# Gated MLP forward on one core: the row-tile and chunk order, the layer norm and a guard pass put in a hand-written order

## The chip, the cores and the metric

One core of a Trainium2 chip. The metric is the device time of one execution in microseconds (us), taken as the median of repeated runs. Engines in the text: PE (matrix multiply; PEld is its weight load), DVE (vector), ACT (scalar, with activation tables), POOL and SP. DMAs are issued by SP (one queue) and by POOL (another), and both queues are served by the core's 16 DMA engines.

## The reference

The forward and backward pass of a block over 2048 rows of width D = 576. Only the first stage of the kernel is touched by the change. What the whole computes:

```python
xn = layernorm(x)                                  # 2048 x 576, eps 1e-5
s  = attention(xn, k_cache, v_cache, wq, wo)       # 32 heads of 128, 2048 keys
h  = sigmoid(xn @ w_gate) * (xn @ w_up)            # F = 4608
g  = silu(h @ w_down)
out = x + s * g
# and the gradients with respect to x, k_cache, v_cache, wq, wo,
# w_gate, w_up, w_down for a given grad_out
```

Everything is bfloat16 in memory; matmuls accumulate in float32.

## The kernel before

**The whole.** The program runs in stages: layer norm and the gate and up projections of the MLP (the stage of this change), the down projection with the derivative of the silu (L425 and following), attention head by head forward and backward, then the weight gradients and the gradient of x. The first stage ends at 377.5 us of the profiled execution, and the down projection follows.

**The tiling of the first stage.** 2048 rows are NT = 16 row tiles of 128. D = 576 is DT = 5 contraction tiles of 128; the last is padded: only 64 rows of it hold data, and the 64 low partitions of the weights' last tile are zeroed (`zlow`, L128, by POOL). F = 4608 is NFC = 9 chunks of 512 columns (`FCH`). For one row tile and one chunk PE runs five matmuls into `g_ps` (L363) and five into `u_ps` (L365), each of 128x512; ACT makes `a_row` = sigmoid(g) (L366), DVE makes `h_row` = u * a (L369). Call this a step. `g_ps` and `u_ps` have three PSUM buffers each. GRP = 3 chunks form a group; there are three groups, and in each the loop runs over all 16 row tiles. At the end of a row tile in a group POOL writes `h_row` and `a_row` (128 x 1536, three buffers each) to `h_d` and `a_d` in HBM (L371, L372).

**Layer norm.** `ln_tile(st)` (L327 to L341) is called two row tiles ahead within the first group. For each row tile it runs the statistics on DVE (L331, L333), a square root on ACT (L335), reciprocal and bias on DVE (L336, L339), the normalization on ACT, in place in `x_all` (L340), five transposes on PE (L58), and a copy of the result into `xnT`, in turn on DVE (L42) and ACT (L40). The square root and the sigmoid lie in different activation tables, and a change between them appears as ACT_TABLE_LOAD in the trace.

**Loads.** SP loads row tiles 0 and 1 of x (L303), then for chunk 0 the five contraction tiles of both weights (L314, L315, ten DMAs), then the other 14 row tiles (L317), then the rest of the weights in column ranges of up to 1536. POOL stores the normalized rows to `xn_d` (L351) and loads the down weights `wd_sb` (L352); in the program both stand at the last row tile of the first group.

**The guard.** The attention stage has a fast path that is valid only if the keys and `wq` are small. A guard computes sums of squares: it loads 84 pieces of 128x1024 (64 of `A_k_cache`, 20 of `wq`) into the space of `x_all`, nine slots, and squares and sums each, odd pieces on ACT (L265), even ones on DVE (L267). `guard_step` issues the load of piece k on SP and the square of piece k - GLA, with GLA = 5. It is called once in each step of the second and third group, between the sigmoid and the product:

```python
                            nc.scalar.activation(a_row[:, cs], g_ps[:], AF.Sigmoid)
                            if grp > 0:
                                guard_step()
                            nc.vector.tensor_tensor(h_row[:, cs], u_ps[:], a_row[:, cs], op=ALU.mult)
```

`guard_end` (L282 to L296) reduces the sums over the partitions through a small tensor in HBM and sets a flag.

**What sets the order.** The order within each engine is not that of the program: a scheduler reorders instructions by priority where dependencies allow. The trace shows it: `wd_sb` is issued at 8.96 us, and the guard's squares begin at 113 us, before the last row tile of the first group is through. Dependencies between engines, and reuse of buffers, are semaphore waits, placed by the framework.

## Time and profile before

| | us |
|---|---|
| median of 5 runs | 5120.81 (5105.55 to 5129.96) |
| the profiled execution | 5134.45 |
| its span, first to last instruction | 5131.7 |
| PE busy | 4952.4 (97%) |
| end of the first stage in it | 377.5 |
| mean granted TensorE clock | 0.99 |

The profile is of one execution. Busy times are sums over instructions; the ends of matmuls are modelled, so a busy PE isn't PE at its peak. In the rows of waits the columns are: who waited for whom, us in total, times, the longest. In the rows of DMA issues: tensors, queue, count, KB of each, and the median us from issue to landing. In the rows by stretch of time each engine has its busy us and its number of instructions.

### The profile page before, as it was taken

To read this page: it belongs to the slowest core of one execution; us is meant where nothing else is said; L and a number is where in the kernel's file an instruction comes from. 1 tells how busy PE (TensorE), PEld (TensorE's weight loads), DVE (VectorE), ACT (ScalarE), POOL (GpSimd) and SP (SyncE) were. 2 spreads that over 40 slices of the span, in tenths; PEclk is the share of its full clock that TensorE was granted. 3 is DMA by queue.
4 is the path that set the end of the run, shared out by engine and by line. 5 is a ranking of instruction groups with operands and counts; after the bars stand their busy time and mean duration, and the time that the engine had idled before them with its cause. 6 is when DMAs were issued, how large, how long until landed. Compare 5 with 4: busy or idle time off the path is not lost.

```text
span 5131.7 us, 127940 instructions
## 1 busy us (share of the span) xinstructions
PE 4952.4 (97%) x53585; PEld 3487.5 (68%) x54480; DVE 2585.8 (50%) x6734; ACT 2602.6 (51%) x4663; POOL 896.6 (17%) x1370
## 2 busy tenths in 40 slices
PE   8899999999999999999999999999899999999999
PEld 3345677777778777777777877777746666555554
DVE  4534556656666666665665666666525444200111
ACT  6521666666667666666666766666513333211000
POOL 1112111111111111111111111111112222211000
PEclk8999999999999999999999999999999999999999
DMA  7648999999999999999999999999986665797976
GB/s 271 234 147 195 177 198 212 208 205 208 206 201 208 214 206 208 206 208 201 215 212 194 211 215 205 209 202 203 210 205 188 188 190 183 221 262 179 174 142 122
DMA packets 2756960, 1031.35 MB, mean 201 GB/s; under 512 B 2663761, under 2 KB 2667986, under 8 KB 2756370
## 3 DMA queue, kind: packets, MB, share of 16 engines
q1 hardware_dynamic: 2659490, 699.97, 73.2%
q0 software_dynamic: 96880, 323.05, 19.3%
q8 instruction: 427, 7.00, 0.6%
q14 instruction: 163, 1.34, 0.1%
HBM read 175.31 MB, written 182.13 MB: 70 GB/s over the span
## 4 chain that ended last, share of the span: by engine, by line
PE 79%; issue 10%; DMA 7%; DVE 2%; POOL 2%; ACT 1%; SPq 0%; POOLq 0%; DVEq 0%; ACTq 0%
PE acc L623 15%; PE acc L564 14%; PE acc L855 12%; PE sp L517 7%; PE acc L1026 6%; PE acc L212 5%; PE dp L587 5%; PE dh L908 3%; PE acct L145 2%; PE u_ps L365 2%; DMA out_dram<-kvo 2%; PE g_ps L363 2%; PE acc L425 2%; PE acc L826 2%; DMA x_all<-in_A_k_cache_dram 1%
## 5 line engine op out<-in xcount | busy, mean ns | idle before, releaser
L535 ACT ACTIVATE Pq<-sp 128x1024 bf16<-128x1024 f32 x1024 | 1048.0, 1024 | 317.7 <-PE sp L517 203.9
L623 PEld LDWEIGHTS <-Pq 128*128 128x128 bf16 x16384 | 1004.9, 98 | 241.8 <-issue 3.4
L594 ACT ACTIVATE t<-dp,negdelta 128x1024 bf16<-128x1024 f32 x512 | 571.6, 1116 | 222.1 <-PE dp L587 168.8
L590 DVE SCALAR_TENSOR_TENSOR Pq<-dp,negdelta,Pq 128x1024 bf16<-128x1024 f32 x512 | 655.0, 1279 | 42.4 <-PE acc L564 38.7
L564 PEld LDWEIGHTS <-PT 128*128 128x128 bf16 x8192 | 502.5, 98 | 129.9 <-DMA PT<-Pq 8.2
L587 PE MATMUL dp<-VT,dOT 128*128 128x512 bf16 x1728 | 542.8, 381 | 32.6 <-DVE Pq L590 32.4
L564 PE MATMUL acc<-Vn,PT 128*128 128x128 bf16 x8192 | 547.5, 219 | 14.6 <-DMA PT<-Pq 7.8
L564 PE MATMUL acc<-Kn,dST 128*128 128x128 bf16 x8192 | 551.6, 219 | 9.4 <-DMA dST<-Pq 5.8
L623 PE MATMUL acc<-dOn,Pq 128*128 128x128 bf16 x8192 | 547.0, 219 | 10.1
L517 PE MATMUL sp<-KQ 128*128 128x512 bf16 x1762 | 548.3, 380 | 2.9 <-ACT Pq L535 2.8
L623 PE MATMUL acc<-Qn,Pq 128*128 128x128 bf16 x8192 | 542.9, 220 | 3.4
L564 PEld LDWEIGHTS <-dST 128*128 128x128 bf16 x8192 | 492.5, 98 | 68.3 <-DMA dST<-Pq 7.6
L595 DVE TENSOR_TENSOR Pq<-t,Pq 128x1024 bf16<-128x1024 bf16 x512 | 354.3, 692 | 359.0 <-ACT t L594 352.2
L604 ACT ACTIVATE dq_n<-acc,rsc 128x128 bf16<-128x128 f32 x512 | 188.3, 368 | 336.7 <-PE acc L564 336.7
L1042 DVE SCALAR_TENSOR_TENSOR junk<-acc,xn_all 128x512 f32<-128x512 f32 (+1 forms) x32 | 13.9, 453 | 642.9 <-ACT dxn L1041 642.9
L637 POOL DMA_DIRECT2D out_dram<-kvo x256 | 140.4, 548 | 1036.5 <-DVE kvo L635 1031.2
L558 POOL DMA_DIRECT2D on_d<-o_n x128 | 97.1, 759 | 741.4 <-DVE junk L576 391.5
L1041 ACT ACTIVATE dxn<-acc 128x512 f32<-128x512 f32 (+1 forms) x32 | 12.8, 406 | 399.6 <-PE acc L1026 392.1
L910 DVE TENSOR_TENSOR du_blk<-dh,ah 128x256 bf16<-128x256 f32 x288 | 120.4, 418 | 188.1 <-PE dh L908 186.0
L635 DVE SCALAR_TENSOR_TENSOR kvo<-acc,part 128x512 bf16<-128x512 f32 x256 | 175.9, 687 | 65.8 <-DMA out_dram<-kvo 37.1
L50 DVE TENSOR_SCALAR o_n<-acc,rinv_all 128x128 bf16<-128x128 f32 x352 | 123.2, 350 | 168.2 <-PE acc L564 168.2
L522 DVE TENSOR_REDUCE rs_all<-rsp 128x1 f32<-128x2 f32 x512 | 78.0, 152 | 256.3 <-ACT Pq L535 254.0
(198 smaller groups left out, 6989.8 us busy)
## 6 DMA issues: line engine op xcount, KB each, us to landing
out_dram<-kvo POOLq DMA_DIRECT2D x256, 128.0 KB, 4.1
h_d<-h_row POOLq DMA_DIRECT2D x48, 384.0 KB, 3.0
a_d<-a_row POOLq DMA_DIRECT2D x48, 384.0 KB, 2.6
ah<-a_d POOLq DMA_DIRECT2D x18, 1024.0 KB, 7.0
ah<-h_d POOLq DMA_DIRECT2D x18, 1024.0 KB, 9.9
du_d<-du_blk POOLq DMA_DIRECT2D x18, 1024.0 KB, 8.7
dg_d<-dg_blk POOLq DMA_DIRECT2D x18, 1024.0 KB, 10.4
x_all<-in_A_k_cache_dram SPq DMA_DIRECT2D x64, 256.0 KB, 6.2
```

The costliest lines, as they stand in the source:

```text
L212: nc.tensor.matmul(av[:, :CH], lhsT=w[:, i, :], rhs=srcT[:, i, cs], start=(i == 0), stop=(i == DT - 1))
L517: nc.tensor.matmul(sp[:, c * CH:(c + 1) * CH], lhsT=hs.QT[:, qt * P:(qt + 1) * P], rhs=hs.KT[:, hf * HW_ + c * CH: hf * HW_ + (c + 1) * CH ...
L535: nc.scalar.activation(Pq[:, hsl], sp[:], AF.Exp, scale=SCALE, accum_out=hs.rsp[:, hf:hf + 1])
L564: nc.tensor.matmul(hs.acc[:, 0, :], lhsT=T[:, kt, :], rhs=rhs[:, kt, :], start=(kt == 0), stop=(kt == NT - 1))
L587: nc.tensor.matmul(dp[:, c * CH:(c + 1) * CH], lhsT=hs.dOT[:, qt * P:(qt + 1) * P], rhs=hs.VT[:, hf * HW_ + c * CH: hf * HW_ + (c + 1) * C ...
L590: nc.vector.scalar_tensor_tensor(Pq[:, hsl], dp[:], hs.negdelta[:, qt:qt + 1], Pq[:, hsl], op0=ALU.add, op1=ALU.mult)
L594: nc.scalar.activation(t[:], dp[:], AF.Identity, bias=hs.negdelta[:, qt:qt + 1], scale=1.0)
L595: nc.vector.tensor_tensor(Pq[:, hsl], t[:], Pq[:, hsl], op=ALU.mult)
L604: nc.scalar.activation(hs.dq_n[:, qt % G4, :], hs.acc[:, 0, :], AF.Copy, scale=hs.rsc[:, qt:qt + 1])
L623: nc.tensor.matmul(self.tile[:, j, :], lhsT=self.slabs[qt][:, kt * P:(kt + 1) * P], rhs=self.rhs[:, qt, :], start=(qt == self.lo), stop=(q ...
L855: nc.tensor.matmul(accs[j][:, :nn], lhsT=lhs[:, st, cols], rhs=rhs[:, st, n0:n0 + nn], start=(st == 0), stop=(st == NT - 1))
L1026: nc.tensor.matmul(self.accs[sl][j][:, :nn], lhsT=ch[:, kk, sl * P:(sl + 1) * P], rhs=wT[:, k0 + kk, n0:n0 + nn], start=(self.k + kk == 0) ...
```

## The change

The nine chunks are walked in five groups: chunk 0 alone, then the pairs (1,2), (3,4), (5,6), (7,8); each group runs over all 16 row tiles. The weights are loaded in the same groups, with one DMA for the four full contraction tiles of a weight and one for the padded one. Seven row tiles of x are loaded (in three DMAs) ahead of the first weights. The zeroing of the padding is split: the first 512 columns on DVE, the rest on POOL.

The layer norm is taken apart into `bn` (statistics), `rstd` (root, reciprocal, bias for a range of row tiles), `norm`, `turn` (transposes) and `put_T` (copy). Roots are taken three times: for row tiles 0 and 1, 2 to 6, and 7 to 15. The block is in `tc.manual_schedule()`: the instructions of each engine keep the order of the program. `xn_d` and `wd_sb` are issued after the first group. The row buffers are 128x1024, four of each.

The guard's ticks are spread over the 128 steps of the pairs, ending 14 steps before the last, with GLA = 7; the square now stands after the product of the step. `guard_end` is split: `guard_reduce`, with the DMAs, follows the last tick.

```diff
@@ -129,7 +129,8 @@
 
     FCH = min(512, F)
     NFC = F // FCH
-    GRP = ldiv(NFC, 3)
+    NB2F = ldiv(NFC - 1, 2) if NFC > 1 else 1
+    groups1 = [(0, 1)] + [(c, c + NB2F) for c in range(1, NFC, NB2F)]
 
     acc_box = [None]
     heads_pre = {}
@@ -238,7 +239,7 @@
         GQ = NT * P // 2
         NGW = -(-HD // GQ)
         NGS = NT * D // GQ
-        GLA = min(5, NGS - 1)
+        GLA = min(7, NGS - 1)
         pieces = [("k", h, hf) for h in range(H) for hf in range(2)] + [("w", i, c) for i in range(DT) for c in range(NGW)]
...
@@ -278,7 +279,9 @@
 
         x_flat = [None]
 
-        def guard_end():
+        gr_box = []
+
+        def guard_reduce():
             gm = gp.tile([P, 2], f32, name="gm", bufs=1)
             ks = gp.tile([P, H], f32, name="ks", bufs=1)
             nc.vector.tensor_reduce(ks[:], ksq[:].rearrange("p (h a) -> p h a", a=2), axis=AX.X, op=ALU.add)
@@ -288,6 +291,10 @@
             nc.sync.dma_start(gd_d[1:2, :].rearrange("o p -> p o"), gm[:, 1:2])
             gr = gp.tile([1, 2, P], f32, name="gr", bufs=1)
             nc.sync.dma_start(gr[:], gd_d[:, :].rearrange("(o a) p -> o a p", o=1))
+            gr_box.append(gr)
+
+        def guard_end():
+            gr = gr_box[0]
             gs = gp.tile([1, 4], f32, name="gs", bufs=1)
             nc.vector.tensor_reduce(gs[:, 0:1], gr[:, 0, :], axis=AX.X, op=ALU.max)
             nc.vector.tensor_reduce(gs[:, 1:2], gr[:, 1, :], axis=AX.X, op=ALU.add)
@@ -299,79 +306,133 @@
         x_all = a0x.tile([P, NT, D], bf, name="x_all")
         x_flat[0] = x_all[:].rearrange("p t d -> p (t d)")
         with tc.tile_pool(name="a1w", bufs=1) as wp:
-            XF = min(2, NT)
-            nc.sync.dma_start(x_all[:, 0:XF, :], x2[0:XF * P, :].rearrange("(t p) d -> p t d", p=P))
-            xn_st = x_all
             wg_sb = wp.tile([P, DT, F], bf, name="wg_sb")
             wu_sb = wp.tile([P, DT, F], bf, name="wu_sb")
-            zlow(wg_sb)
-            zlow(wu_sb)
-            WSPL = GRP * FCH
-            bounds = [0, FCH] + list(range(WSPL, F + 1, WSPL)) if WSPL > FCH else list(range(0, F + 1, WSPL))
-            for bi in range(len(bounds) - 1):
-                c0, c1 = bounds[bi], bounds[bi + 1]
-                for i, (d0, kd) in enumerate(dts):
-                    nc.sync.dma_start(wg_sb[P - kd:, i, c0:c1], B_w_gate[d0:d0 + kd, c0:c1])
-                    nc.sync.dma_start(wu_sb[P - kd:, i, c0:c1], B_w_up[d0:d0 + kd, c0:c1])
-                if bi == 0 and NT > XF:
+
+            def zero_cols(eng, c0, c1):
+                if KPAD:
+                    for w_ in (wg_sb, wu_sb):
+                        eng.memset(w_[:LO, DT - 1, c0:c1], 0.0)
+
+            def load_w(w_, src, c0, c1):
+                nf = DT - 1 if KPAD else DT
+                if nf:
+                    nc.sync.dma_start(w_[:, :nf, c0:c1], src[:nf * P, c0:c1].rearrange("(i p) c -> p i c", p=P))
+                if KPAD:
+                    nc.sync.dma_start(w_[LO:, nf, c0:c1], src[nf * P:, c0:c1])
+
+            XF = min(7, NT)
+            for xs, xe in ((0, 1), (1, 2), (2, XF)):
+                if xs < xe:
+                    nc.sync.dma_start(x_all[:, xs:xe, :], x2[xs * P:xe * P, :].rearrange("(t p) d -> p t d", p=P))
+            zero_cols(nc.vector, 0, FCH)
+            zero_cols(nc.gpsimd, FCH, F)
+            for gi, (fa, fz) in enumerate(groups1):
+                load_w(wg_sb, B_w_gate, fa * FCH, fz * FCH)
+                load_w(wu_sb, B_w_up, fa * FCH, fz * FCH)
+                if gi == 0 and NT > XF:
                     nc.sync.dma_start(x_all[:, XF:, :], x2[XF * P:, :].rearrange("(t p) d -> p t d", p=P))
             FMAX = nc.vector.BN_STATS_FMAX
             nchunk = 1
             while D % nchunk != 0 or D // nchunk > FMAX:
                 nchunk += 1
             with tc.tile_pool(name="a0", bufs=3) as sb0, tc.tile_pool(name="a0ps", bufs=2, space=PSUM) as ps0, \
-                    tc.tile_pool(name="a1r", bufs=3) as rows, \
-                    tc.tile_pool(name="a1ps", bufs=3, space=PSUM) as ps:
-
-                def ln_tile(st):
-                    xt = x_all[:, st, :]
+                    tc.tile_pool(name="a1r", bufs=4) as rows, \
+                    tc.tile_pool(name="a1ps", bufs=3, space=PSUM) as ps, tc.manual_schedule():
+                mv_all = sb0.tile([P, NT, nc.vector.BN_AGGR_DIM], f32, name="mv_all", bufs=1)
+                nbias = sb0.tile([P, NT], f32, name="nbias", bufs=1)
+
+                def bn(st):
                     stats = sb0.tile([P, nchunk, nc.vector.BN_STATS_DIM], f32, name="stats")
-                    xr = xt.rearrange("p (c f) -> p c f", c=nchunk)
+                    xr = x_all[:, st, :].rearrange("p (c f) -> p c f", c=nchunk)
                     for c in range(nchunk):
                         nc.vector.bn_stats(stats[:, c, :], xr[:, c, :])
-                    mv = sb0.tile([P, nc.vector.BN_AGGR_DIM], f32, name="mv")
-                    nc.vector.bn_aggr(mv[:], stats[:])
-                    std = sb0.tile([P, 1], f32, name="std")
-                    nc.scalar.activation(std[:], mv[:, 1:2], AF.Sqrt, bias=eps_t[:], scale=1.0)
-                    nc.vector.reciprocal(rstd_all[:, st:st + 1], std[:])
-                    xn_t = xn_st[:, st, :]
-                    nbias = sb0.tile([P, 1], f32, name="nbias")
-                    nc.vector.scalar_tensor_tensor(nbias[:], mv[:, 0:1], -1.0, rstd_all[:, st:st + 1], op0=ALU.mult, op1=ALU.mult)
-                    nc.scalar.activation(xn_t, xt, AF.Identity, bias=nbias[:], scale=rstd_all[:, st:st + 1])
-                    transpose_to(nc, ps0, xn_t, D, xnT, st * P, ident, alt)
-
-                LA = 2
-                for st in range(min(LA, NT)):
-                    ln_tile(st)
-                for grp in range(NFC // GRP):
+                    nc.vector.bn_aggr(mv_all[:, st, :], stats[:])
+
+                def rstd(a, b):
+                    y = rstd_all[:, a:b]
+                    std = sb0.tile([P, NT], f32, name="std")
+                    nc.scalar.activation(std[:, a:b], mv_all[:, a:b, 1], AF.Sqrt, bias=eps_t[:], scale=1.0)
+                    nc.vector.reciprocal(y, std[:, a:b])
+                    nc.vector.scalar_tensor_tensor(nbias[:, a:b], mv_all[:, a:b, 0], -1.0, y, op0=ALU.mult, op1=ALU.mult)
+
+                pts = {}
+
+                def norm(st):
+                    xt = x_all[:, st, :]
+                    nc.scalar.activation(xt, xt, AF.Identity, bias=nbias[:, st:st + 1], scale=rstd_all[:, st:st + 1])
+
+                def turn(st):
+                    pts[st] = ps0.tile([P, 8, P], bf, name="pt", tag="tr")
+                    for i in range(DT):
+                        c0 = min(i * P, D - P)
+                        nc.tensor.transpose(pts[st][:, i, :], x_all[:, st, c0:c0 + P], ident[:])
+
+                def put_T(st, eng):
+                    alt.copy(xnT[:, :, st * P:(st + 1) * P], pts.pop(st)[:, :DT, :], eng=eng)
+
+                LA = min(2, NT)
+                L1 = min(7, NT)
+                for st in range(LA):
+                    bn(st)
+                rstd(0, LA)
+                for st in range(LA):
+                    norm(st)
+                    turn(st)
+                    put_T(st, "v")
+                for st in range(LA, L1):
+                    bn(st)
+                if LA < L1:
+                    rstd(LA, L1)
+                    norm(LA)
+                bn_left = list(range(L1, NT))
+                nstep = sum(NT * (fz - fa) for fa, fz in groups1[1:])
+                ntot = len(pieces) + GLA
+                step = 0
+                for gi, (fa, fz) in enumerate(groups1):
                     for st in range(NT):
-                        if grp == 0 and st + LA < NT:
-                            ln_tile(st + LA)
-                        if grp == 0 and st == NT - 1:
-                            nc.gpsimd.dma_start(xn_d[:, :].rearrange("(t p) d -> p t d", p=P), xn_st[:])
-                            nc.gpsimd.dma_start(wd_sb[:], B_w_down.rearrange("(t p) d -> p t d", p=P))
+                        if gi == 0:
+                            if st + LA + 1 < NT:
+                                norm(st + LA + 1)
+                            if st + LA < NT:
+                                turn(st + LA)
                         srows = slice(st * P, (st + 1) * P)
-                        a_row = rows.tile([P, GRP * FCH], bf, name="a_row")
-                        h_row = rows.tile([P, GRP * FCH], bf, name="h_row")
-                        for c in range(GRP):
-                            fc = grp * GRP + c
+                        a_row = rows.tile([P, NB2F * FCH], bf, name="a_row")
+                        h_row = rows.tile([P, NB2F * FCH], bf, name="h_row")
+                        for fc in range(fa, fz):
                             fs = slice(fc * FCH, (fc + 1) * FCH)
-                            cs = slice(c * FCH, (c + 1) * FCH)
+                            cs = slice((fc - fa) * FCH, (fc - fa + 1) * FCH)
                             g_ps = ps.tile([P, FCH], f32, name="g_ps")
                             u_ps = ps.tile([P, FCH], f32, name="u_ps")
                             for i, (d0, kd) in enumerate(dts):
                                 nc.tensor.matmul(g_ps[:], lhsT=xnT[:, i, srows], rhs=wg_sb[:, i, fs], start=(i == 0), stop=(i == DT - 1))
                             for i, (d0, kd) in enumerate(dts):
                                 nc.tensor.matmul(u_ps[:], lhsT=xnT[:, i, srows], rhs=wu_sb[:, i, fs], start=(i == 0), stop=(i == DT - 1))
+                            if gi == 0 and st + LA < NT:
+                                put_T(st + LA, "s")
                             nc.scalar.activation(a_row[:, cs], g_ps[:], AF.Sigmoid)
-                            if grp > 0:
-                                guard_step()
                             nc.vector.tensor_tensor(h_row[:, cs], u_ps[:], a_row[:, cs], op=ALU.mult)
-                        cols = slice(grp * GRP * FCH, (grp + 1) * GRP * FCH)
-                        nc.gpsimd.dma_start(h_d[srows, cols], h_row[:])
-                        nc.gpsimd.dma_start(a_d[srows, cols], a_row[:])
-            while gk[0] < len(pieces) + GLA:
+                            if gi:
+                                step += 1
+                                while gk[0] < min(ntot, ntot * step // max(1, nstep - 14)):
+                                    guard_step()
+                                    if gk[0] == ntot:
+                                        guard_reduce()
+                            elif bn_left:
+                                for _ in range(min(3 if st == 0 else 2, len(bn_left))):
+                                    bn(bn_left.pop(0))
+                                if not bn_left:
+                                    rstd(L1, NT)
+                        nn = (fz - fa) * FCH
+                        nc.gpsimd.dma_start(h_d[srows, fa * FCH:fz * FCH], h_row[:, :nn])
+                        nc.gpsimd.dma_start(a_d[srows, fa * FCH:fz * FCH], a_row[:, :nn])
+                    if gi == 0:
+                        nc.gpsimd.dma_start(xn_d[:, :].rearrange("(t p) d -> p t d", p=P), x_all[:])
+                        nc.gpsimd.dma_start(wd_sb[:], B_w_down.rearrange("(t p) d -> p t d", p=P))
+            while gk[0] < ntot:
                 guard_step()
+                if gk[0] == ntot:
+                    guard_reduce()
             guard_end()
             NHV = min(NT, NT * D // (FT * P))
             hT_first = [x_flat[0][:, b * FT * P:(b + 1) * FT * P].rearrange("p (f s) -> p f s", s=P) for b in range(NHV)]
```

## The prediction

> **What bounds the kernel now.** I read the page first (engines, the 40 slices), then the busy time by stretch of the MLP forward stage, then PE's waits in it, then the chain of waits in its first 40 us, then the POOL issues with their times to landing.
>
> ```profile
> span 5131.7 us, 127940 instructions
> PE 4952.4 (97%) x53585; PEld 3487.5 (68%) x54480; DVE 2585.8 (50%) x6734; ACT 2602.6 (51%) x4663; POOL 896.6 (17%) x1370
> ```
>
> PE bounds the whole. The diff touches only the stage that ends at 377.5 us, where the last `u_ps` matmul is over and the down projection (L425) begins with no gap. By stretch of that stage (columns: PE, PEld, DVE, ACT, POOL busy, granted clock, DMA share, GB/s):
>
> ```profile
> 0.00:38.50 38.50, 16.83 (x53) 6.45 (x55) 11.41 (x45) 11.87 (x17) 10.37 (x9) 0.69 0.96 326
> 38.50:109.00 70.50, 69.90 (x347) 32.84 (x353) 32.39 (x77) 60.91 (x82) 12.77 (x23) 0.98 0.61 227
> 109.00:215.00 106.00, 83.17 (x360) 35.84 (x365) 72.29 (x128) 65.05 (x121) 12.71 (x24) 0.97 0.89 293
> 215.00:377.50 162.50, 161.49 (x736) 73.43 (x750) 51.92 (x75) 44.78 (x75) 26.70 (x50) 1.00 0.37 136
> ```
>
> Only the last row is dense. The first is starved with DMA full; the third has PE at 83 of 106 us with DMA again near full. PE's waits up to 378 us say on what:
>
> ```profile
> PE u_ps L365 <- DVE h_row L369: 12.0, 12, 5.2
> PE g_ps L363 <- DMA wg_sb<-in_B_w_gate_dram: 10.8, 4, 7.1
> PE g_ps L363 <- ACT a_row L366: 10.6, 11, 1.9
> PE pt L58 <- ACT x_all L340: 6.7, 1, 6.7
> PE u_ps L365 <- DMA wu_sb<-in_B_w_up_dram: 3.8, 4, 1.8
> ```
>
> The weight waits belong to the first stretch: row tile 0 needs three chunks, and the 5.2 MB load of `wd_sb`, issued at 9 us, shares the engines. The waits on `a_row` and `h_row` belong to the third: there the guard's squares (L265, L267) sit in front of the evacuations on ACT and DVE and wait for their own data:
>
> ```profile
> ACT x_all L265 <- DMA x_all<-in_A_k_cache_dram: 20.6, 15, 5.9
> DVE x_all L267 <- DMA x_all<-in_A_k_cache_dram: 16.9, 12, 4.9
> ```
>
> **The ledger.** The chain shows five 512-column matmuls per 1.08 us, 0.216 us each. The stage has 9 chunks x 16 row tiles x 10 = 1440: 310.8 us. A row tile's five transposes put 0.27 us between two such groups; 16 make 4.3. Together 315.1, so 377.5 - 315.1 = 62.4 us are lost now. The change leaves the matmuls alone; the question is what is lost afterwards.
>
> **Start, up to the first dense matmul.** Before chunk 0 is complete the new SP queue has seven row tiles (1.0 MB) and 1.2 MB of weights, in 7 issues at 0.43 to 0.58 us. At the 341 to 389 GB/s of the starved stretch 2.2 MB take 6.5 us after 3 us of first latency: about 10 us, and `wd_sb` no longer competes. The layer norm is then last. On DVE: tile 0 is there at 3.7 us as now, two tiles of statistics at 0.8 to 1.1 each, root (ACT 0.3), reciprocal and bias (0.16 each), norm 0.86 each, transposes on a cold PE 0.75, copies 0.49: about 9.9 us. Then five tiles of statistics at 0.8 (4.0), root, reciprocal, bias (0.9), norm of tile 2 (0.86), its transposes (0.75): the first matmul at 16.5 us. The zeroing of 512 columns moves to DVE: 64x4608 costs POOL 3.9 us, so 512 of them are some 0.4 for each weight, on a DVE that waits for x until 3.7. Lost: 16.5. PE is cold there (clock 0.50 in the starved stretch; the first seven matmuls at 38.5 us took 3.19 instead of 1.5): 2.1 more.
>
> **First pass, 16 steps of one chunk.** PE has 2.16 + 0.27 = 2.43 us a step. ACT has norm 0.86, copy 0.69, sigmoid 0.59 = 2.14: just under, with no table load between. DVE has the product 0.69 and two or three statistics of 0.8 to 1.0 in the first four steps, over 2.43, which three PSUM buffers absorb. The statistics of tile 15 end near 31.4 us; the second root, reciprocal and bias give tile 7's norm at 33.1, but PE is at its transposes at 30.6: 2.5 us lost. The sigmoid's table load (1.28) stands before the next norm: 0.9. Sum 3.4. The x tiles behind those statistics land near 13 us, so that cover is wide. The pass ends at about 16.5 + 2.1 + 34.5 + 3.8 + 3.4 = 60.3 us.
>
> **ACT table loads.** The trace has 26 in the stage, at 1283 ns; after it 4. That frees 28 us of ACT. The Trainium skill's page "ScalarE: Activation LUTs" ("What ACT_TABLE_LOAD costs") gives the same load and adds a drain, 2.66 us a switch: 58.5 us freed, and 1.4 us more at the one reload on PE's path. In this trace the root starts 0.02 us after its load, so I take 1.28. Either way ACT's freed time counts for PE only in what PE waits; that is in the sums above.
>
> **Stores.** The rows are written in 160 POOL issues instead of 96, of 128 and 256 KB instead of 384. At 0.54 us an issue that is 35 us more of POOL, which is busy 63 of 377 us. "DMA: Bandwidth & Descriptors" ("Anatomy of one DMA — SWDGE (gpsimd) path") speaks against it: about 2 us fixed for each DMA, so 64 more are 128 us in series. The rows landing in 2.6 us show that they overlap; a buffer returns only after four steps of 2.43 or 4.3 us. I count zero; without that cover it would show as waits of `a_row`.
>
> **The moved load: a new wait.** The queue of POOL is where I expect the loss. `xn_d` (2.3 MB) and `wd_sb` (5.2 MB) now go out together after the first pass, at about 63 to 66 us, ahead of the first stores of the paired chunks. Now `xn_d` goes out at 98.59 us and these are its landing and that of the `h_d` store issued at 102.0:
>
> ```profile
> xn_d<-x_all POOLq DMA_DIRECT2D x1, 2304.0 KB, 9.4
> h_d<-h_row POOLq DMA_DIRECT2D x1, 384.0 KB, 7.0
> ```
>
> One ends at 108.0, the other at 109.0, though a store alone takes 2.6 to 3.5: it lands behind what was queued before it. With `wd_sb` in front (27.1 us to land at the start), the first `a_row` of the pairs lands late. `xn_d` is over near 72.5 us; that also releases the guard's first nine loads (nine slots, SP has nothing else to wait for), 2.4 MB which share the engines with the 5.3 of `wd_sb`: 7.7 MB at 360 GB/s and 2 us, 95 to 96 us, and the store some 1 us later. ACT needs that buffer back for the fifth row tile of the pair: 60.3 + 4 x 4.32 + 1.3 = 78.9. ACT stands until 96.5. PE has three PSUM buffers: it goes on for three steps from 77.6, to 84.1, and resumes at 97.1: 13 us. Bounds: zero if stores overtake, 17 if `wd_sb` takes 27 us from the end of `xn_d`. After a 5.2 us wait at 207.6 the next five matmuls took 2.29 us instead of 1.08, so I add 2 for a cold PE.
>
> **Guard.** 84 pieces plus a lead of 7 are 91 ticks in 114 of 128 steps instead of one each step: 256 KB per 2.7 us is 97 GB/s, the stores about 122, below the 360. A piece has 7 ticks, 19 us, against 5 to 7 to land. The 22.6 us of PE waits on `a_row` and `h_row` go; 1 stays as margin. The final reduction (9.4 and 2.2 us of DMA) ends inside the last 14 steps, 30 us.
>
> **Sum.** 315.1 + 16.5 + 2.1 + 3.4 + 13 + 2 + 1 = 353.1 us, against 377.5: 24.4 less. The later stages start alike and are bound by PE; I count zero. The profiled execution took 5134.45 (span 5131.7 and 2.8 around), 13.6 above the median of the five runs; from it 5110, from the median **5096**. About 0.3% (15 us) is what a measurement of this kernel tells from no change.
>
> **Rivals.** (1) *The stores overtake, or the buffers suffice*: no 13 + 2, so 39 less, 5081. Against it stands the landing pair above; for it, that PE has slack in PSUM. (2) *The freed time comes back later*, or first-pass waits on norm are longer (each ACT instruction has a semaphore to wait for, and 2.14 of 2.43 is tight; 0.3 more a step is 5 us): 8 to 12 less, 5110. (3) *Slower: the clock stays at half for the whole first pass.* PE never runs without a wait on norm, so 14 steps take 10 x 0.43 + 0.5 = 4.8 us: 33 more, net 9 more, 5130. It decides from the point where ACT's step exceeds PE's warm step 2.43. Against it: between 109 and 215 us PE waits 23 us in short pieces and is granted 0.97. (4) *The change doesn't do what it says*: the order by hand binds only within the block; if the loads before it were reordered, chunk 0 comes late by up to the 38 us of now, and the gain is about zero.
>
> **How the numbers follow.** Forecast 0.52 (its own range 5086 to 5108 with the block between 5 and 17 us and runs scattering by 8), rival 1 0.20, rival 2 0.15, rival 3 0.06, rival 4 0.07. Faster by over 0.3% needs below 5105: nine tenths of the forecast, all of rival 1, a third of rival 2: 0.72. Slower: 0.09 from the upper end of rivals 3 and 4. The rest, 0.19, is within 0.3%. The range takes rival 1 at its end and most of rival 2: 5074 to 5120.
>
> **What would show it.** First dense matmul near 16 to 18 us, not 38. Four table loads. One wait of PE near 84 us of 5 to 17, `u_ps` or `g_ps` on `a_row`, and ACT's `a_row` released by DMA `a_d`. Almost no waits of L265 and L267 on DMA. Last matmul of the stage near 353. A first pass past 75 us, or several `a_row` waits on stores, would prove it wrong, and so would a loss after the stage.

## The result and the profile after

The changed kernel takes 5102.24 us (median of 22 runs, 5088.33 to 5116.69) against 5124.55 for the kernel before (43 runs). The ratio is 0.9958, 95% interval 0.9949 to 0.9967: 21.5 us less, between 17 and 26. The profiled execution took 5111.12 us, its span is 5109.3. PE's last `u_ps` matmul of the first stage ends at 360.0 us instead of 377.5, and the down projection starts at 361.2 instead of 378.3.

The busy time by stretch of the stage (columns: PE, PEld, DVE, ACT, POOL busy, granted clock, DMA share, GB/s):

```profile
0.00:16.00 16.00, 2.40 (x17) 1.60 (x18) 8.73 (x31) 5.35 (x8) 7.59 (x8) 1.00 0.91 286
16.00:64.00 48.00, 44.28 (x240) 21.71 (x244) 19.94 (x46) 32.46 (x48) 19.11 (x34) 1.00 0.78 264
64.00:120.00 56.00, 45.29 (x197) 19.99 (x200) 19.24 (x29) 16.01 (x29) 11.93 (x21) 0.91 0.87 310
120.00:200.00 80.00, 79.63 (x365) 36.32 (x371) 42.78 (x69) 37.77 (x68) 20.11 (x38) 1.00 0.64 217
200.00:300.00 100.00, 99.53 (x456) 45.30 (x463) 52.68 (x85) 46.98 (x84) 24.93 (x47) 1.00 0.63 215
300.00:360.00 60.00, 51.38 (x223) 22.74 (x227) 21.15 (x39) 17.87 (x31) 11.79 (x22) 0.91 0.58 142
```

The starved start is over at 16 us, and from 120 to 300 us PE is dense although the guard runs there. Most of what is lost after the start sits in two rows, the third and the last, each with the clock down to 0.91. PE's waits of more than 2 us up to 375 us name both:

```profile
PE pt L369 <- ACT x_all L363: 17.1, 4, 6.9
PE g_ps L408 <- ACT a_row L413: 10.3, 1, 10.3
PE u_ps L410 <- DVE h_row L414: 8.4, 1, 8.4
```

Before, PE waited on `a_row` and `h_row` 23 times, 22.6 us together; now it waits once on each, and long. The first of the three rows holds the start (6.7 and 6.9 us ahead of the transposes of tiles 0 and 2) and two waits in the first pass, 2.7 and 0.8. The first long wait is that of a store. These are the POOL issues between 60 and 66 us (the last column is us to landing):

```profile
wd_sb<-in_B_w_down_dram POOLq DMA_DIRECT2D x1, 5184.0 KB, 28.1
xn_d<-x_all POOLq DMA_DIRECT2D x1, 2304.0 KB, 10.3
h_d<-h_row POOLq DMA_DIRECT2D x1, 256.0 KB, 27.0
a_d<-a_row POOLq DMA_DIRECT2D x1, 256.0 KB, 27.3
h_d<-h_row POOLq DMA_DIRECT2D x1, 128.0 KB, 2.0
a_d<-a_row POOLq DMA_DIRECT2D x1, 128.0 KB, 2.0
```

The 128 KB stores went out ahead of `wd_sb` and landed in 2.0 us; the 256 KB ones behind it took 27. The timeline shows what waited for them:

```profile
91.97 0.54 POOL L428 DMA_DIRECT2D a_d<-a_row  x1 [13.09 <-DMA wd_sb<-in_B_w_down_dram]
93.40 1.08 ACT L413 ACTIVATE a_row<-g_ps 128x512 bf16<-128x512 f32 x2 [16.60 <-DMA a_d<-a_row]
94.05 0.58 PE L408 MATMUL g_ps<-wg_sb,xnT 128*128 128x512 bf16 x1 [10.32 <-ACT a_row L413]
```

The second long wait is at the end of the stage (timeline of SP, DVE and PE from 314 us):

```profile
314.50 11.97 SPq L440 DMA_TRANSPOSE x_all<-h_d  x2
326.57 0.52 SPq L290 DMA_DIRECT2D gd_d<-gm  x1
327.20 0.37 SPq L291 DMA_DIRECT2D gd_d<-gm  x1
339.26 0.29 SPq L293 DMA_DIRECT2D gr<-gd_d  x1
...
341.81 0.27 DVE L299 TENSOR_REDUCE gs<-gr 1x1 f32<-1x128 f32 x1 [13.40 <-DMA gr<-gd_d]
...
343.52 2.29 PE L410 MATMUL u_ps<-wu_sb,xnT 128*128 128x512 bf16 x5 [8.35 <-DVE h_row L414]
```

`guard_end` stands outside the hand-ordered block. The scheduler put its five small DVE operations four products behind the reduction and ahead of the last ten products of the stage, and put the two DMA transposes of `h_d` ahead of the reduction's own DMAs on SP. DVE stands 13.4 us for `gr`, with the products behind it; PE runs out of PSUM buffers and waits 8.4.

The change did not bring this wait. It was in the kernel before, in the list of all waits and in PE's timeline:

```profile
DVE gs L292 <- DMA gr<-gd_d: 10.2, 1, 10.2
212.79 2.29 PE L365 MATMUL u_ps<-wu_sb,xnT 128*128 128x512 bf16 x5 [5.20 <-DVE h_row L369]
```

There the scheduler had put the same five operations three products behind the reduction. DVE stood 10.2 us, and PE's longest wait on `h_row`, the 5.2 us, was for the products behind them. The changed kernel keeps this wait and makes it longer.

After both waits PE is cold, that is, its matmuls take about twice as long for a while: the 15 matmuls from 94.05 us take 5.7 us instead of 3.2, those from 343.52 take 5.55. The ledger closes: 315.1 of work, 15.5 to the first dense matmul, 2.1 cold there, 3.5 in the first pass, 10.3 + 2.4 and 8.4 + 2.3 for the two stalls, sum 359.6, measured 360.0.

The down projection gained a little too. From its first matmul to the first `sp` matmul of the attention it takes 151.9 us against 154.0. Before, the load of `grad_out` was issued at 387.40 us, behind the head loads of K and V (386.34 and 386.87); a product on DVE waited 7.6 us for it, and PE 1.9 us for that product. Now it is issued at 364.16, K at 372.34; DVE's wait is 0.7, and PE has none there.

### The profile page after: what moved, and what is told of

The parts are those of the page before. It is cut to its first block, busy times and chain, and to the rows that moved or that the text cites. A ratio compares the mean times of both kernels' runs of the same rounds, so it can differ in the third digit from the quotient of the medians.

```text
span 5109.3 us, 128009 instructions
## 1 busy us (share of the span) xinstructions
PE 4940.1 (97%) x53584; PEld 3486.4 (68%) x54480; DVE 2582.1 (51%) x6704; ACT 2576.0 (50%) x4634; POOL 929.4 (18%) x1434
## 4 chain that ended last, share of the span: by engine, by line
PE 83%; issue 8%; DMA 5%; DVE 2%; POOL 1%; ACT 1%; POOLq 0%; SPq 0%; DVEq 0%; ACTq 0%
PE acc L684 15%; PE acc L625 15%; PE acc L916 13%; PE sp L578 7%; PE acc L1087 7%; PE dp L648 6%; PE acc L213 6%; PE dh L969 3%; PE acc L486 3%; PE acct L146 2%; PE u_ps L410 2%; PE g_ps L408 2%; PE acc L887 2%; DMA out_dram<-kvo 2%; DVE Pq L651 1%
## 5 line engine op out<-in xcount | busy, mean ns | idle before, releaser
L656 DVE TENSOR_TENSOR Pq<-t,Pq 128x1024 bf16<-128x1024 bf16 x512 | 354.3, 692 | 357.0 <-ACT t L655 350.1
L648 PEld LDWEIGHTS <-dOT 128*128 128x128 bf16 x2048 | 163.9, 98 | 68.7 <-issue 46.6
```

The source lines that it names most:

```text
L648: nc.tensor.matmul(dp[:, c * CH:(c + 1) * CH], lhsT=hs.dOT[:, qt * P:(qt + 1) * P], rhs=hs.VT[:, hf * HW_ + c * CH: hf * HW_ + (c + 1) * C ...
L656: nc.vector.tensor_tensor(Pq[:, hsl], t[:], Pq[:, hsl], op=ALU.mult)
```

## The experiments

The end of the stage can be read from one trace to about 1 us (378.3 and 377.2 in two traces of the kernel before); the whole time cannot. In the 14 traces of this case (both kernels, a second one of before, eleven variants) the rest, from the first `sp` matmul to the end of the span, took between 4573 and 4603 us, 4599.4 and 4582.1 in two traces of the same kernel before. So the stage end (start of the down projection) carries the verdicts, and the ratios, each to runs of before from the same set, stand beside it with their 95% intervals.

| kernel | stage end, us | ratio to before |
|---|---|---|
| before; again | 378.3; 377.2 | 1 |
| after | 361.2 | 0.9958 (0.9949 to 0.9967) |
| e1_wd_sp | 346.3 | 0.9932 (0.9916 to 0.9947) |
| e2_ge_last | 350.3 | 0.9937 (0.9923 to 0.9952) |
| e3_both | 338.0 | 0.9917 (0.9897 to 0.9938) |
| e4_wd_first | 354.3 | 0.9958 (0.9938 to 0.9979) |
| e5_no_hand_order | 370.1 | 0.9982 (0.9963 to 1.0001) |
| e6_three_chunks | 343.2 | 0.9885 (0.9863 to 0.9907) |
| e7_guard_each_step | 345.7 | 0.9936 (0.9916 to 0.9957) |
| e8_root_each_row | 370.8 | 0.9940 (0.9918 to 0.9961) |
| e9_one_chunk_best | 338.5 | 0.9923 (0.9903 to 0.9942) |
| e10_three_chunks_best | 337.5 | 0.9895 (0.9873 to 0.9917) |
| e11_before_wd_sp | 364.0 | 0.9970 (0.9959 to 0.9982) |

**e1_wd_sp: is it the queue or the bandwidth?** The load leaves POOL's queue and goes out on SP behind the guard's ninth piece.

```diff
                                     guard_step()
+                                    if gk[0] == NGS:
+                                        nc.sync.dma_start(wd_sb[:], B_w_down.rearrange("(t p) d -> p t d", p=P))
...
-                        nc.gpsimd.dma_start(wd_sb[:], B_w_down.rearrange("(t p) d -> p t d", p=P))
```

> The load of wd_sb goes out on SP's queue behind the guard's first nine loads instead of on POOL's queue; same bytes at the same moment. Queue theory (a store lands behind what POOL queued before it): ACT's wait of 16.6 us for the a_row store and PE's wait of 10.3 us near 84 us vanish, with the cold clock after them 12 us of the stage, which ends near 349 instead of 361.2; ratio to before 0.993 to 0.994 (after: 0.9958). Rival, bandwidth (7.7 MB of loads in flight keep any store late): the wait stays at 8 us or more and the ratio at 0.995 to 0.996.

The stall near 84 us is gone, and the stage ends 14.9 us earlier. PE's waits of more than 2 us up to 400 us:

```profile
PE pt L369 <- ACT x_all L363: 16.5, 3, 6.9
PE u_ps L410 <- DVE h_row L414: 5.8, 1, 5.8
```

The stretch from 64 to 120 us, in the columns used above:

```profile
64.00:120.00 56.00, 55.74 (x256) 25.39 (x260) 25.95 (x40) 22.67 (x41) 13.99 (x26) 1.00 0.97 354
```

PE is dense at 354 GB/s, more than the 310 of the kernel with the stall. The 256 KB stores issued from 66 to 100 us land in 5.3 to 5.6 us (medians) instead of 27, although the load, issued at 77.75 us on SP, runs beside them. The 12.7 us of the stall and 2.6 less of waiting at the end make the 14.9 to within 0.4. The queue was the cause, not the bandwidth.

**e2_ge_last: the wait at the end.** `guard_end` becomes the last statement within the hand-ordered block. The loop ahead of it moves in with it; it has nothing left to do there, since the ticks are over 14 steps before the end.

```diff
-            while gk[0] < ntot:
-                guard_step()
-                if gk[0] == ntot:
-                    guard_reduce()
-            guard_end()
+                while gk[0] < ntot:
+                    guard_step()
+                    if gk[0] == ntot:
+                        guard_reduce()
+                guard_end()
```

> Only the five small DVE operations of guard_end move behind the last product of the stage. Theory (DVE stands 13.4 us for gr with five row tiles' products queued behind it): PE's wait of 8.4 us near 335 and about 2.3 of cold clock after it go, the stage ends near 351, ratio 0.9935 to 0.9945. Rival, the wait is only moved: something else, the load of the transposed h or the store of the last rows, ends the stage at 358 or later, ratio over 0.9955.

DVE's order differs in nothing but these operations, which now follow the last product. Of PE's two long waits one is left:

```profile
PE g_ps L408 <- ACT a_row L413: 10.3, 1, 10.3
```

The stage ends at 350.3, 10.9 us earlier. The rival falls: nothing took its place. The two DMA transposes (13.3 us here) still go ahead of the reduction's DMAs on SP, so it was the place on DVE that cost PE the time, not the order on SP.

**e3_both.**

> Both edits. If the two stalls are separate and nothing takes their place the stage ends near 339 and the ratio is 0.9905 to 0.992. Rival, the next stage gives it back (it waits for the transposed h, for grad_out or for the head loads): the stage ends near 339, but the down projection's first matmuls wait for 5 us or more and the ratio is 0.993 or more.

PE's waits of more than 0.5 us up to 400 us:

```profile
PE pt L369 <- ACT x_all L363: 16.5, 3, 6.9
PE acc L487 <- DVE h_row L414: 0.9, 1, 0.9
```

Both long waits are gone, 23.2 us of stage end, and the down projection takes 151.9 us as in the changed kernel: nothing is given back. What is left is the start and the first pass.

**e4_wd_first: the load at the start.** It stands ahead of the first load of x.

```diff
+            nc.gpsimd.dma_start(wd_sb[:], B_w_down.rearrange("(t p) d -> p t d", p=P))
...
-                        nc.gpsimd.dma_start(wd_sb[:], B_w_down.rearrange("(t p) d -> p t d", p=P))
```

> The load of wd_sb is issued by POOL first of all, so it shares the engines with x and the first weights, as it did before the change. Theory: no stall near 84; 2.2 MB of x and chunk 0 take 12 us more or less beside it and are there at about 15, just when the layer norm is through (15.5), so the start moves by 0 to 2 us and the ratio is 0.993 to 0.9945. Rival, this load was what starved the start before the change: the first dense matmul comes 5 us or more later than 15.5, statistics wait for x, and the ratio is 0.9955 or more.

Half a miss. The first dense matmul comes at 15.56 us, as expected, and there is no stall near 84. But x was to be a little late, and it was very late: tiles 7 to 15 took 23.0 us to land instead of 10.3, DVE stood 7.2 us before their statistics, and PE waited 2.9 and 7.3 us in the first pass. The stage ends 6.9 us earlier than in the changed kernel, about half of what the stall had cost. The queues from 8 to 20 us (columns: packets, MB, share of the engines) show why the estimate failed: the two queues did not share evenly.

```profile
q0 software_dynamic: 800, 3.69, 84.4%
q1 hardware_dynamic: 800, 0.79, 19.9%
```

POOL's one load moved 3.69 MB while SP's queue, with x and weights waiting in it, moved 0.79. Both had 800 packets; POOL's carry 4.6 KB each, SP's 1.0 (worked out from the row).

**e5_no_hand_order: the loops without the order.**

```diff
-                    tc.tile_pool(name="a1ps", bufs=3, space=PSUM) as ps, tc.manual_schedule():
+                    tc.tile_pool(name="a1ps", bufs=3, space=PSUM) as ps:
```

> The changed kernel with the hand order taken off: same loops, same calls, the scheduler orders each engine by priority again. It then puts the load of wd_sb before the first store on POOL, near 8 us. Theory (the order, not the loops, removed the waits): x tiles 7 to 15 land after 25 us as in the run that issued wd_sb first, the guard's squares run ahead in front of sigmoids and products, PE waits 15 us or more on a_row and h_row, and the stage ends at 365 or later, ratio 0.996 or more. Rival (the loops and the guard's pace did it): no bunching, no stall near 84, the stage ends at 350 or before, ratio 0.9945 or less.

PE's four largest waits up to 400 us:

```profile
PE pt L369 <- ACT x_all L363: 11.3, 2, 9.4
PE g_ps L408 <- ACT a_row L413: 9.4, 9, 3.3
PE u_ps L410 <- DVE flag_i L303: 7.1, 1, 7.1
PE u_ps L410 <- DVE h_row L414: 5.4, 5, 3.6
```

The short waits are back: the scheduler does not keep the spread pace that the loops ask for. The guard's squares run from 71 to 146 us (97 to 319 in the changed kernel), and in that time PE waits 11.5 us on `a_row` and `h_row`; the other 3.3 of these two rows came at 39 us, before any square. `guard_end` blocks the products here too (7.1). One part of the expectation missed: x tiles 7 to 15 landed 9.6 us after their issue, and the first dense matmul came at 13.3 us, so POOL's early load of `wd_sb`, issued at 8.1 us here and behind x (at 1.3 us and ahead of x in e4), did not hold the start.

The stage ends at 370.1, 7.6 us before the old kernel (377.75, the mean of its two traces), where the changed kernel has 16.6. So a little more than half of the change's gain at the stage end is its order, the two stalls already taken off. By the whole time this kernel is not told apart from the one before (the interval reaches 1.0001).

**e6_three_chunks and e7_guard_each_step**, each on e3_both. In e6 chunk 0 is still loaded by itself, and the row buffers are three of 128x1536.

```diff
-    groups1 = [(0, 1)] + [(c, c + NB2F) for c in range(1, NFC, NB2F)]
+    NB2F = ldiv(NFC, 3)
+    groups1 = [(c, c + NB2F) for c in range(0, NFC, NB2F)]
```

> On top of the version without the two stalls (wd_sb behind the guard's first nine loads on SP, guard_end last): the chunks are walked in threes over all row tiles as before the change, with one chunk of weights loaded first; row buffers 128x1536, three. Theory (one chunk first is worth little once wd_sb is out of the way): chunk 0 is there at 10 us and chunks 1 and 2 at about 20, when row tile 0 needs chunk 1, so 0 to 2 us more at the start; the 3.5 us of waits on norm in the first pass go, since three chunks stand between two row tiles; stage end 335 to 341 against 338.0, ratio 0.9905 to 0.993. Rival (the one-chunk pass is what hides the weights): PE waits 8 us or more for weights of chunks 1 and 2, stage end 345 or later.

```diff
-        GLA = min(7, NGS - 1)
+        GLA = min(5, NGS - 1)
...
-                                while gk[0] < min(ntot, ntot * step // max(1, nstep - 14)):
+                                while gk[0] < min(ntot, step):
```

> On top of the version without the two stalls: the guard ticks once in each step from the first step of the pairs, with a lead of 5, as before the change; only the hand order holds it to that pace. Theory (the scheduler's bunching, one piece per us, was what stalled ACT and DVE, not one piece per step): 118 GB/s of guard and 122 of stores fit under 360, PE waits 3 us or less more, stage end 338 to 341. Rival (the pace of 0.8 and the lead of 7 are needed): squares wait for their pieces, PE waits 10 us or more on a_row and h_row between 64 and 260, stage end 348 or later, ratio 0.9935 or more.

Both ended later than expected, and the traces show the same wait. PE's waits besides those of the start and the first pass, in e6, then in e7:

```profile
PE g_ps L409 <- ACT a_row L414: 6.5, 1, 6.5
PE u_ps L411 <- DMA wu_sb<-in_B_w_up_dram: 1.8, 1, 1.8
```

```profile
PE g_ps L408 <- ACT a_row L413: 6.6, 1, 6.6
```

One wait of 6.5 us each: on SP the guard's tenth piece queues behind `wd_sb`, and at the faster tick of these two (91 ticks in 82 steps in e6, one in each step in e7) it is not there when ACT comes to it; ACT stood 11.8 us for a piece in both. This is read from the traces; no run under the hand order has the fast tick with the load elsewhere. It would make the wait one of my edit and the tick together, not of the tick alone. Nothing else of the tick shows in e7: PE's only other waits are those of the start and the first pass. And the rival of e6, that one chunk first is needed to hide the weights, falls at this start: 1.8 us of wait for weights.

**e8_root_each_row**, on e3_both.

```diff
-                    rstd(LA, L1)
+                    rstd(LA, LA + 1)
...
+                                rstd(st + LA + 1, st + LA + 2)
                                 norm(st + LA + 1)
...
-                                    rstd(L1, NT)
```

> On top of the version without the two stalls: a root for each row tile just before its norm, so 13 more pairs of table loads in the first pass. Theory: ACT's step becomes 2.14 + 0.30 + 2 x 1.28 = 5.0 us and two crossings to DVE of 0.4 to 0.8 are added, against 2.43 of PE: 13 steps lose 2.6 to 3.4 each, the first pass is 33 to 44 us longer, less the 3.5 of waits on norm that go: stage end 367 to 379, ratio 0.998 to 1.0005; the batched roots are then worth more than all else. Rival (table loads hide behind waits, as before the change): less than 10 us, stage end 348 or before.

The stage ends at 370.8, 32.8 us later, with 14 waits on norm. PE's waits, and then the stretch from 16 to 64 us:

```profile
PE pt L369 <- ACT x_all L363: 39.9, 14, 6.7
```

```profile
16.00:64.00 48.00, 30.55 (x132) 12.54 (x134) 15.76 (x51) 39.66 (x49) 8.71 (x16) 0.82 0.71 219
```

ACT is busy 40 of 48 us and PE 31. The period of a step is 6.2 us (the sigmoid's table load comes at 23.87 and at 30.09). At the stage end, within the hand order and the one-chunk walk, taking the roots together is worth more than any other part tested. The whole time does not follow: the stage says 0.998, the interval ends at 0.9961. The profiled execution took 5119.61 us, which is 0.998 of before's 5130.40 and fits its stage; the median of the five is 5099.50. Likewise e6 is faster as a whole (0.9885) than its stage allows (0.993), and so is e10 below (0.9895 against 0.992), while e5, e7 and e9 agree with their stages. Only the profiled executions show where the time goes; why the others of these three are quicker is open.

**e9_one_chunk_best and e10_three_chunks_best: the rest of the start.** Both have `guard_end` last and `wd_sb` on SP right behind the weights, where in the changed kernel SP stands idle 36.9 us for `xn_d`; e10 has the chunks in threes as well. The cut shows what both share at the start.

```diff
-                for st in range(LA, L1):
-                    bn(st)
-                if LA < L1:
-                    rstd(LA, L1)
-                    norm(LA)
+                bn(LA)
+                rstd(LA, LA + 1)
+                norm(LA)
+                for st in range(LA + 1, L1):
+                    bn(st)
+                rstd(LA + 1, L1)
                 bn_left = list(range(L1, NT))
+                for _ in range(3):
+                    bn(bn_left.pop(0))
...
-                                for _ in range(min(3 if st == 0 else 2, len(bn_left))):
+                                for _ in range(min(3, len(bn_left))):
```

> guard_end last; wd_sb on SP right behind the last weights, where SP's queue stands idle until xn_d; the root of row tile 2 taken by itself so that PE starts before the statistics of tiles 3 to 6, and three more tiles of statistics ahead of the first product. Expected: first dense matmul at 11.9 instead of 15.5, the 3.5 us of waits on norm in the first pass 1 or less, no wait on a_row or h_row over 1 us; stage end 331 to 334 against 338.0, ratio 0.990 to 0.9915. Rival: wd_sb at 36 to 55 us delays the stores of the first pass behind shared engines and PE waits 3 us or more on a_row; stage end 336 or later.

> The same with the chunks in threes. Theory (the walk of one chunk first is not needed): start at 11.9, row tile 0 waits up to 4 us for the weights of chunk 1 (there at about 20, needed at 16), nothing else; stage end 330 to 335, within 3 us of the one-chunk version. Rival (the one-chunk walk hides the weights): PE waits 8 us or more for weights, stage end 339 or later.

Both missed their stage end. In e9 the first dense matmul comes at 11.82 us as expected, but nothing of the 3.7 us arrives at the end (338.5, as e3). The chain moved on: the last root is now in ACT's order after the second sigmoid, where it stands for DVE's statistics, and the norms of the next tiles stand behind it (timelines of ACT and PE in e9):

```profile
25.24 1.28 ACT L356 ACT_TABLE_LOAD   x1 [5.17 <-DVE mv_all L351]
...
27.65 0.72 PE L370 MATMUL pt<-ident,x_all 128*128 128x128 bf16 x5 [6.00 <-ACT x_all L364]
```

PE waits 6.0 us there, and is cold again. DVE's sixteen tiles of statistics, at some 0.93 us each, all stand ahead of that root. In e10, PE waits 2.5 and 2.6 us for weights, more than in e6, whose start was later; the ten matmuls behind the second wait take 4.2 us instead of 2.16, and 0.5 more is waited on `a_row`. It ends at 337.5, with the old walk of three. So the walk of one chunk first is not what brings the gain at the stage end. No version here ends the stage below 337.5; e3, e9 and e10 beat both kernels, and are not told apart by these runs. The lowest whole times are those of the two versions in threes, e6 and e10, by more than their stages explain.

**e11_before_wd_sp: the old kernel with one edit.** The load goes out on SP, behind the loads of the weights.

```diff
+            nc.sync.dma_start(wd_sb[:], B_w_down.rearrange("(t p) d -> p t d", p=P))
...
-                            nc.gpsimd.dma_start(wd_sb[:], B_w_down.rearrange("(t p) d -> p t d", p=P))
```

> The kernel before the change with one edit: the load of wd_sb is issued on SP behind the weights instead of on POOL. Theory (POOL's early load starved the start): 5.9 MB of x and three chunks are there at about 20 us, the dense matmuls begin at 18 to 23 instead of 38.5, the stage ends 10 to 18 us earlier than 377.5 (the bunched guard stays), ratio 0.9965 to 0.998. Rival (the weights themselves bound the start, 13 MB at 370 GB/s is 36 us): the start stays past 30 us and the ratio at 0.999 or more.

The stage ends at 364.0, 13.7 us earlier than in the two traces of before; by itself one line gives most of what the whole change gave at the stage end (16.6). The waits for weights fall from 14.6 us to 4.7, while the bunched waits of the guard (11.8 and 10.8) stay. The weights were not the bound.

**e12_before_again.**

> The kernel before once more, for its trace: the first one has 152.7 us from the first output projection of the attention to the first dh matmul, the changed kernel 145.6. If the change made that difference the second trace shows 151 to 154 too; if it is the spread between executions, 144 to 150.

145.0 us: the 7 us in the attention's projection are spread between executions, not the change's. The stage end (377.2) and the down projection (154.3 us) are close to those of the first trace. The down projection takes 153.8 in e11 and 151.9 or 152.0 in all ten variants of the changed kernel, so these differences are the change's.

## Why the prediction held, and where it did not

The forecast was 24.4 us less; measured are 21.5, between 17 and 26, and in the traces 18.8 up to the first `sp` matmul (the mean of before's two, 531.9, against 513.1). The stage itself came out 6.9 us later than forecast (360.0 against 353.1). By its own steps:

- **Start.** 16.5 forecast, 15.5 measured; the layer norm was last, as said. Cold 2.1 and 2.1.
- **First pass.** Waits 3.4 forecast (2.5 and 0.9), 3.5 measured (2.7 and 0.8). The pass ended at 59.8, forecast 60.3.
- **ACT table loads.** 1.28 us each. There are four, as forecast. The drain that the Trainium skill's page "ScalarE: Activation LUTs" ("What ACT_TABLE_LOAD costs") adds does not show: in e8 the root at 27.07 us starts 0.01 after its load, the sigmoid at 25.16 likewise, and the load at 25.78 starts 0.02 after that sigmoid ends.
- **Stores.** Zero, rightly: before `wd_sb`, they land in 2.0 us and nobody waits. The 2 us for each DMA that the Trainium skill's page "DMA: Bandwidth & Descriptors" ("Anatomy of one DMA — SWDGE (gpsimd) path") states is there as the time of one to land, and the stores overlap: they are issued 0.54 us apart.
- **The moved load.** The mechanism is right, and e1 shows that it is the queue. `xn_d` landed at 72.5, as forecast; `wd_sb` at 91.5 instead of 95 to 96; ACT resumed at 93.4 instead of 96.5; PE waited 10.3 instead of 13 (and 2.4 cold, forecast 2). The 3 us are the engines' rate: from 80 to 100 us they moved 376 GB/s, and the forecast had put 360 GB/s and 2 us on top.
- **Guard.** The step that failed is the last one: that the final reduction costs nothing because it "ends inside the last 14 steps". It did end there, at 342.8 us of 360.0; the conclusion was wrong. The forecast costed its DMAs (9.4 and 2.2 us) and found them shorter than 30 us, but what counts is who stands behind the operation that waits for them: `guard_end` was outside of the hand-ordered block, so its place on DVE was the scheduler's, ahead of ten products. It was left in the 1 us of margin and cost 10.7 (8.4 and 2.3 cold); e2 takes 10.9 off. The trace before had shown it: of the 22.6 us of waits that were to go, 5.2 were for this reduction, and the forecast used that very wait, at 207.6 us, only as an example of a cold PE.
- **The rest of the guard.** The waits of L265 and L267 on their pieces are gone. In e7 the old pace brings back none of the short waits under the hand order, only the one of 6.6 us, so the order and not the slower pace removed them.
- **The later stages.** Counted as zero; the down projection gained 2.1. PE's wait behind the `grad_out` load (1.9) is gone; no run tests that order alone.

In the stage, the missed 10.7 was offset in part by the start (1.0), the shorter stall (2.7, less 0.4 of cold) and the unused margin (1), which leaves the 6.9 to within 0.5; the down projection gave back 2.1. That the whole came out so near is partly luck: errors of one sign met errors of the other. Rival 3, half clock through the first pass, did not come: from 21.5 us on, five matmuls take 1.08 us. Rival 1 fell with the stall, and rival 4 in part only: the order did bind within the block, and failed at its edge.

## What to carry to other kernels

Cost a moved transfer by what its queue holds behind it and by when the buffers of those must come back, not by whether the engines have bandwidth: here a large load ahead of small stores on one queue kept their buffers for as long as it ran. When an order is fixed by hand, look at both edges of the fixed block, since what stands outside may be placed into it: here five small operations that waited for a DMA stopped all the products queued behind them on DVE. When waits are counted as gone, ask of each long one what ended it, since one of them may have another cause than the rest. And before a loop order is credited with a gain, move the one load that competes at the start; here that single line by itself brought 13.7 us where the whole change brought 16.6.

## What the runs showed of the hardware

- Two queues with work did not share the engines evenly. From 8 to 20 us of e4, 3.69 MB of POOL's load went through against 0.79 of SP's, with 800 packets each.
- POOL itself stood for its own load: by the profile the `a_d` issue at 91.97 us waited 13.1 us for `wd_sb`, and no store went out in between. Why the issue waits for it is open.
- 8 to 10 us without a matmul cost 2.3 to 2.5 us of half clock afterwards (15 matmuls in 5.55 to 5.7 us instead of 3.2), nearly the same at 94 and at 343 us. A shorter wait can cost as much: in e10 two waits of 2.5 and 2.6 us, with five matmuls between them, were followed by ten that took 4.2 us instead of 2.16.
